# Turning K on VectorE in 32x32 blocks in a one-token decode attention layer

## The chip, the cores and the metric

The kernel runs on one NeuronCore of a Trainium2 chip. Its time is the device time of one execution in microseconds (us). A core has TensorE (PE: matmuls and, as PEld, their weight loads), VectorE (DVE), ScalarE (ACT), GpSimd (POOL) and SyncE (SP), each with its own program in order; they meet through semaphores. 16 DMA engines move data between HBM and the on-chip SBUF; matmuls write to the eight banks of PSUM.

## What is computed

Two tokens (batch B = 2) attend over a window of the last W = 2048 of 8192 cached positions, with 16 query heads on 8 key heads of width 256. The result is gated by a small two-layer network. Cut to what matters:

```python
xn = layernorm(x)                                  # x: 2 x 1 x 448, all bfloat16
q = (xn @ wq).reshape(B, 1, 16, 256)               # wq: 448 x 4096
k, v = k_cache[:, :, -2048:], v_cache[:, :, -2048:]  # 2 x 8 x 2048 x 256, two query heads each
p = softmax(q @ k.T * 256 ** -0.5)
s = (p @ v).reshape(B, 1, 4096) @ wo               # wo: 4096 x 448
g = silu(relu(xn @ w1) @ w2)                       # w1: 448 x 1792, w2: 1792 x 448
out = x + s * g
```

## The kernel before

The work is cut into four units (u = 0 to 3), each one token and four key heads. K of a unit and V of a unit are 4 MB each; a partition holds NT = 64 positions of one head with 256 values each, 32 partitions to a head. Every load is issued by SP, in this order: two rows' share of wq, K0, the rest of wq, K1, V0, w1, w2, and, as buffers come free, K2, V1, K3, V2, V3 in two parts (`load_v` with cuts at 48 and 64 of 64), then wo in the parts of `WO_PARTS` (L106, L530; 32 groups of rows in all). There are two buffers each for K and V; `load_k` (L206) waits for the last transpose of the unit two before, `load_v` (L209) for its last PV matmul (V1 for q's matmuls), since wq lies in a V buffer and wo in a K buffer.

The program is laid out by hand: each helper appends operations to the lists of the engines, and the order of the calls (L510 to the end) is the order on each engine. Semaphore waits follow from the dependencies given.

- `do_T` (L294) turns K for the score matmuls: 16 chunks a unit, each four TensorE transposes of 128x128 4-byte words (two bfloat16 each) into a PSUM bank, moved to `kt` by DVE (L309) or, for 7 of 16, ACT (L311).
- `do_S` (L313) makes the scores in bank `sbk`: 32 matmuls a unit, in groups of four that lie side by side on the array, each with the stationary `qz` (32 columns) and a moving operand of 512 columns. All heads' queries meet all rows, and what doesn't belong is masked later.
- `softmax` (L326): maximum over each row (`rm4`), a mask for other heads' columns (`far`, giving `rmm`), maximum again (`rm`), the maximum per head by a small transpose on TensorE (`mrow`, `mall`, `bias`), the shift by it with a second mask (`s_sb`, L351), exp on ACT (`e_sb`, sum in `ssum`), four transposes on TensorE, a copy to `pt`, and the reciprocal of the sum (`gs` matmul, `rs`).
- `do_PV` (L378) multiplies `pt` with V: 32 matmuls a unit, for unit u-1 put into the gaps of unit u's softmax by `gaps` (L499). `idle_work` (L481) puts filler matmuls into the gaps whose result nobody reads. `attend_scale`, `attend_turn` and `attend_spread` (L391 to L411) scale the result (`o_sb`), turn it (`at_exp`) and write it as the stationary `at_z` of the last product.
- `do_q` (L418) makes q once K0 has been turned. `do_H`, `do_hT`, `do_F` (L441 to L463) are the gating network, between units 1 and 2.
- At the end 128 matmuls of 8x112 (four for each of 32 row groups of wo) add up in `obk`, two DVE operations apply the gate and the residual, and ACT issues the store.

Matmuls are issued by one helper, so most of them have the line L281.

Of the kernel before, what the change touches and what calls it, by code (L numbers as in the profile page):

```python
# [76 lines left out]
def bass_recurrent_scan__sliding_block_cached__dense_activation_relu__decode_kernel(  # L77
# [23 lines left out]
    NCHUNK = NT // 4  # L101
# [4 lines left out]
    WO_PARTS = [8, 8, 6, 4, 4, 2]  # L106
# [5 lines left out]
    NTB = 5  # L112
    ON_ACT = (1, 3, 5, 8, 10, 12, 14)
    FAR = -1.0e30
    LOW = -30000.0

    es = contextlib.ExitStack()
    with es:
# [18 lines left out]
        own = named("own", [128, 4], F32)  # L137
        far = named("far", [128, 4], F32)
        low4 = named("low4", [128, 4], F32)
        low = named("low", [128, 512], F32)  # L140
        fold = named("fold", [128, 32], BF)
        fold16 = named("fold16", [128, NWO], BF)
        fold8 = named("fold8", [128, 8], F32)
# [9 lines left out]
        qz = named("qz", [128, 2 * NU * 64], BF)  # L153
        h_n = named("h_n", [128, FC // 4], BF)
        h_z = named("h_z", [128, 14 * GAP], BF)
# [5 lines left out]
        rm4 = named("rm4", [128, 4], F32)  # L161
        rmm = named("rmm", [128, 4], F32)
# [4 lines left out]
        s_sb = named("s_sb", [128, 512], F32)  # L167
        e_sb = named("e_sb", [128, 512], BF)
# [9 lines left out]
        kt = [named(f"kt{i}", [128, 1024], BF) for i in range(NCHUNK)]  # L178

        tb = [psum(f"tb{i}", [128, 1024], BF) for i in range(NTB)]  # L180
        sbk = psum("sbk", [128, 512], F32)
        obk = psum("obk", [128, 512], F32)
        mb16 = psum("mbk", [128, 1024], BF)
        mbk = mb16[:, :].bitcast(F32).tensor
# [48 lines left out]
        p_qz = pr.op(POOL, lambda e: e.memset(qz[:, :], 0.0), [p_one])  # L233
        p_z = [pr.op(POOL, lambda e, t=t: e.memset(t[:, :], 0.0)) for t in (h_z, at_z)][-1]

        a_z = [pr.op(ACTE, lambda e, t=t: e.memzero(t[:, :])) for t in (obk,)][-1]
# [26 lines left out]
        def fold16_op(e):  # L263
            with nc.allow_low_precision("zeros and ones"):
                return e.tensor_reduce(out=fold16[:, :], in_=view(ident, 0, [[1, NWO], [NWO, 8]]), axis=AX.X, op=ALU.add)
        v_fold16 = pr.op(DVE, fold16_op)
        v_f8 = pr.op(DVE, lambda e: e.tensor_reduce(
            out=fold8[:, :], in_=view(ident, 0, [[1, 8], [8, 16]]), axis=AX.X, op=ALU.add))
        v_own = pr.op(DVE, lambda e: e.tensor_reduce(
            out=own[:, :], in_=view(fold8, 0, [[2, 4], [1, 2]]), axis=AX.X, op=ALU.add), [v_f8])  # L270
        v_far = pr.op(DVE, lambda e: e.tensor_scalar(
            out=far[:, :], in0=own[:, :], scalar1=1.0, scalar2=-FAR, op0=ALU.subtract, op1=ALU.mult), [v_own])
        v_low4 = pr.op(DVE, lambda e: e.tensor_scalar(
            out=low4[:, :], in0=own[:, :], scalar1=1.0, scalar2=-LOW, op0=ALU.subtract, op1=ALU.mult), [v_own])
        v_low = pr.op(DVE, lambda e: e.tensor_copy(
            view(low, 0, [[4, 128], [1, 4]]), view(low4, 0, [[0, 128], [1, 4]])), [v_low4])
        v_gs = pr.op(DVE, lambda e: e.tensor_copy(
            view(gsum, 0, [[8, 16], [1, 8]]), view(fold8, 0, [[0, 16], [1, 8]])), [v_f8])
# [11 lines left out]
        st["mbk"] = v_xr  # L290

        evac, last_S = {}, {}

        def do_T(u, i):  # L294
            n_th = NCHUNK * u + i
            bank, src = tb[n_th % NTB], kbuf[u % 2]
            src_f, bank_f = src[:, :].bitcast(F32), bank[:, :].bitcast(F32)
            deps = [d_k[u], p_idf, evac.get(n_th - NTB)]
            for n in range(4):
                lo = (4 * i + n) * (DH // 2)  # L300
                o = pr.op(PE, lambda e, n=n, lo=lo: e.matmul(  # L301
                    bank_f[:, n * 128:(n + 1) * 128], lhsT=src_f[:, lo:lo + 128], rhs=ident_f[:, :],
                    start=True, stop=True, is_transpose=True), deps)
                deps = []
            st["T", u] = o
            dst = kt[i]
            deps = [o, last_S.get(n_th - NCHUNK)]
            if i not in ON_ACT:
                evac[n_th] = pr.op(DVE, lambda e: e.tensor_copy(dst[:, :], bank[:, :]), deps)  # L309
            else:  # L310
                evac[n_th] = pr.op(ACTE, lambda e: e.activation(dst[:, :], bank[:, :], ACT.Copy), deps)  # L311

        def do_S(u, g):  # L313
            deps = [st["q"]] + ([st.get(("shift", u - 1))] if g == 0 else [])
            for par in range(2):
                lo = 64 * (2 * u + par) + 24 - 8 * g
                for i in range(4):
                    o = pr.op(PE, mm(sbk[32 * i:32 * i + 32, :], qz[:, lo:lo + 32], view(kt[4 * g + i], par, [[2, 512]]),
                                     g == 0 and par == 0, g == 3 and par == 1, tile_position=(0, 32 * i)),
                              deps + [evac[NCHUNK * u + 4 * g + i]])  # L320
                    deps = []
            for i in range(4):
                last_S[NCHUNK * u + 4 * g + i] = o
            st["S", u] = o

        def softmax(u, fill=()):  # L326
            fill = list(fill)

            def meanwhile():
                if fill:  # L330
# [3 lines left out]
            v = pr.op(DVE, lambda e: e.tensor_reduce(  # L334
                out=rm4[:, :], in_=view(sbk, 0, [[1, 4], [4, 128]]), axis=AX.X, op=ALU.max), [st["S", u]])
            v = pr.op(DVE, lambda e: e.tensor_tensor(out=rmm[:, :], in0=rm4[:, :], in1=far[:, :], op=ALU.add), [v, v_far])
            v = pr.op(DVE, lambda e: e.tensor_reduce(out=rm[:, :], in_=rmm[:, :], axis=AX.X, op=ALU.max),  # L337
                      [v, st.get(("rmT", u - 1))])
# [4 lines left out]
                out=mrow[0:1, :], in_=view(mbk, 0, [[1, 8], [8, 16]], n=1), axis=AX.X, op=ALU.max, negate=True),  # L343
# [3 lines left out]
                view(mall, 0, [[8, 16], [1, 8]], n=1), view(mrow, 0, [[0, 16], [1, 8]], n=1)),  # L347
                [v, st.get(("bias", u - 1))])
            m = st["bias", u] = pr.op(PE, mm(mbk_ap(128, 1), mall[0:1, :], one_f[0:1, :], True, True), [v, p_one])
            v = st["mbk"] = pr.op(DVE, lambda e: e.tensor_copy(bias[:, :], mbk_ap(128, 1)), [m])  # L350
            v = st["shift", u] = pr.op(DVE, lambda e: e.scalar_tensor_tensor(  # L351
                out=s_sb[:, :], in0=sbk[:, :], scalar=bias[:, 0:1], in1=low[:, :], op0=ALU.add, op1=ALU.min),
                [v, v_low, st.get(("exp", u - 1))])
            meanwhile()
            a = st["exp", u] = pr.op(ACTE, lambda e: e.activation(  # L355
                e_sb[:, :], s_sb[:, :], ACT.Exp, accum_out=ssum[:, 0:1]),
                [v, st.get(("Pt", u - 1)), st.get(("gs", u - 1))])
            deps = [a, st["mbk"]]
            for j in range(4):
                o = pr.op(PE, lambda e, j=j: e.matmul(  # L360
                    mb16[:, 512 + 128 * j:640 + 128 * j], lhsT=e_sb[:, 128 * j:128 * j + 128],
                    rhs=ident[:, :], start=True, stop=True, is_transpose=True), deps)
                deps = []
            st["Pt", u] = o
            v = st["pt", u] = pr.op(DVE, lambda e: e.tensor_copy(  # L365
                view(pt[u % 2], 0, [[256, 2], [16, 16], [8, 2], [1, 8]]),
                view(mb16, 512, [[256, 2], [8, 16], [128, 2], [1, 8]])), [o, st.get(("PV", u - 2))])
            meanwhile()
            m = st["gs", u] = pr.op(PE, mm(mbk_ap(130, 1), gsum[:, :], ssum[:, 0:1], True, True), [v_gs, a, v])
            st["rs", u] = st["mbk"] = pr.op(DVE, lambda e: e.reciprocal(rs[:, u:u + 1], mbk_ap(130, 1)), [m])  # L370
            assert not fill

        obk_last = tb[3][:, :].bitcast(F32).tensor
# [4 lines left out]
        def do_PV(u, gs=range(4)):  # L378
            bank, src, p = out_bank(u), vbuf[u % 2], pt[u % 2]
            for g in gs:  # L380
                deps = [next(d for hi, d in d_v[u] if hi >= 16 * g + 16), st["pt", u], a_z if u < NU - 1 else st["tb3"], st["obk"] if u < NU - 1 else None]
                for a in range(2):
                    for i in range(4):
                        lo = (16 * g + 4 * i + 2 * a) * DH
                        o = pr.op(PE, mm(bank[32 * i:32 * i + 16, :],
                                         p[:, 256 * a + 64 * i + 16 * g:256 * a + 64 * i + 16 * g + 16], src[:, lo:lo + 2 * DH],
                                         g == 0 and a == 0, g == 3 and a == 1, tile_position=(0, 32 * i)), deps)
                        deps = []
            st["PV", u] = o
# [28 lines left out]
        def do_q():  # L418
# [10 lines left out]
            deps = [v, v_xr]  # L429
            for n in range(4):  # L430
                o = pr.op(PE, lambda e, n=n: e.matmul(
                    mb16[:, 128 * n:128 * n + 128], lhsT=view(q_n, 256 * (n // 2) + n % 2, [[2, 128]]),
                    rhs=ident[:, :], start=True, stop=True, is_transpose=True), deps)
                deps = []
            for b in range(2):
# [45 lines left out]
        def idle_work(n):  # L481
            wbk = tb[2][:, :].bitcast(F32).tensor
            deps = [st["q"], p_id]
            for _ in range(n):
                pr.op(PE, mm(view(wbk, 0, [[1, 512]]), ident[:, :], qz[:, :], True, True), deps)
                deps = []
# [106 lines left out]
```

## Time and profile before

| | us |
|---|---|
| median of 13 runs | 112.37 (112.11 to 113.86) |
| the profiled execution | 112.13 |
| its span (first to last instruction) | 110.3 |
| PE busy / PEld busy | 79.4 / 55.1 |
| DVE busy / ACT busy | 49.4 / 35.9 |

The profile is of one execution. The span is cut into 40 slices; a row has one digit for each, the busy share in tenths. A group of instructions is named by line, engine, operation and out<-in tiles; behind the bar stand its busy time, the mean duration of one in ns, and the engine's idle time just before it with what ended it. Matmuls overlap, so their durations are longer than their spacing. "The chain" follows the work that ended last back through what released each step. From the same trace come the records of when each transfer's last piece had landed, and of the TensorE clock that the throttle granted (1.0 or 0.5; mean 0.967 here).

### The profile page before, as it was taken

The numbers are of one execution on the slowest core, as the hardware profiler recorded it, in microseconds if no ns is written. First come the engines' busy times: TensorE is split into PE (matmuls) and PEld (weight loads), VectorE is DVE, ScalarE is ACT, GpSimd is POOL, SyncE is SP. The second block draws the span as 40 slices with busy tenths as digits, with TensorE's granted clock in tenths as the row PEclk, the third lists the DMA queues.
The fourth block names the chain that finished last, engine by engine and source line by source line (L and its number), as shares of the span: only waits on it lengthen the run. The fifth ranks groups of instructions, "written<-read, shape, count | busy, mean of one in ns | idle before, by whom it ended". The sixth has DMA issues, their size and how long they took to land.

```text
span 110.3 us, 1971 instructions
## 1 busy us (share of the span) xinstructions
PE 79.4 (72%) x867; PEld 55.1 (50%) x867; DVE 49.4 (45%) x114; ACT 35.9 (33%) x44; POOL 2.3 (2%) x12
## 2 busy tenths in 40 slices
PE   0010039998766999858489999857399985898991
PEld 0000039993312977323389877322397741335881
DVE  2292005485254575464400976463256655454001
ACT  4930004685002468402000858302046771200000
POOL 6200000000000000000000000000000000000000
PEclk9999999999999999999958999999859999999999
DMA  3989989998999899999999999999999999999930
GB/s 72 500 380 463 475 361 453 493 416 380 416 505 404 380 416 418 404 491 416 478 428 386 428 475 416 386 463 463 392 416 463 395 428 416 385 424 414 395 138 7
DMA packets 2908, 44.24 MB, mean 401 GB/s; under 512 B 338, under 2 KB 468, under 8 KB 1364
## 3 DMA queue, kind: packets, MB, share of 16 engines
q1 hardware_dynamic: 2864, 44.11, 94.4%
q8 instruction: 7, 0.11, 0.4%
q10 hardware_dynamic: 36, 0.01, 0.0%
q14 instruction: 1, 0.01, 0.0%
HBM read 44.11 MB, written 0.00 MB: 400 GB/s over the span
## 4 chain that ended last, share of the span: by engine, by line
PE 40%; DMA 37%; DVE 14%; SPq 3%; ACT 2%; issue 2%
DMA kbuf<-in_A_wo_dram 24%; PE tb L301 20%; DMA kbuf<-in_A_k_cache_dram 13%; PE sbk L281 6%; PE obk L281 4%; PE tb L281 4%; SPq L36 3%; DVE kt L309 2%; PE mbk L281 2%; DVE s_sb L351 2%; ACT e_sb L355 2%; DVE rm L334 2%; PE mbk L360 1%; DVE mrow L342 1%; PE mbk L339 1%
## 5 line engine op out<-in xcount | busy, mean ns | idle before, releaser
L301 PE MATMUL tb<-ident_f,kbuf 128*128 128x128 f32 x256 | 35.8, 300 | 10.6 <-DMA kbuf<-in_A_k_cache_dram 10.6
L301 PEld LDWEIGHTS tb<-ident_f,kbuf 128*128 128x128 f32 x256 | 32.0, 156 | 15.0 <-DMA kbuf<-in_A_k_cache_dram 10.7
L311 ACT ACTIVATE kt<-tb 128x1024 bf16<-128x1024 bf16 x28 | 27.4, 1023 | 26.9 <-PE tb L301 26.7
L309 DVE COPY kt<-tb 128x1024 bf16<-128x1024 bf16 x36 | 24.7, 690 | 23.3 <-PE tb L301 23.1
L281 PE MATMUL sbk<-kt,qz 128*32 128x512 bf16 x128 | 11.0, 393 | 1.6 <-DVE kt L309 1.1
L355 ACT ACTIVATE e_sb<-s_sb 128x512 bf16<-128x512 f32 x4 | 2.5, 629 | 21.4 <-DVE s_sb L351 21.4
L281 PE MATMUL obk<-vbuf,pt 128*16 128x512 bf16 x96 | 7.4, 379 | 0.0
L281 PE MATMUL obk<-kbuf,at_z 128*8 128x112 bf16 x128 | 7.0, 213 | 0.4 <-DMA kbuf<-in_A_wo_dram 0.2
L281 PEld LDWEIGHTS obk<-kbuf,at_z 128*8 128x8 bf16 x128 | 6.3, 87 | 1.0 <-DMA kbuf<-in_A_wo_dram 0.9
L281 PE MATMUL tb<-qz,ident 128*128 128x512 bf16 x20 | 6.2, 382 | 0.0
L281 PEld LDWEIGHTS sbk<-kt,qz 128*32 128x32 bf16 x128 | 2.7, 94 | 5.4 <-DVE kt L309 2.1
L281 PE MATMUL mbk<-ident,xg 2*128 2x2 bf16 x7 | 0.3, 164 | 6.6 <-DVE xg L246 6.6
L334 DVE TENSOR_REDUCE rm<-sbk 128x4 f32<-128x512 f32 x4 | 2.8, 692 | 4.3 <-PE sbk L281 4.3
L281 PE MATMUL tb<-wf,h_z 128*8 128x112 bf16 x56 | 4.3, 260 | 0.5 <-DVE h_z L460 0.5
L281 PEld LDWEIGHTS tb<-wf,h_z 128*8 128x8 bf16 x56 | 4.2, 110 | 0.5 <-issue 0.5
L365 DVE COPY pt<-mbk 128x512 bf16<-128x512 bf16 x4 | 1.7, 424 | 5.0 <-PE mbk L360 5.0
L281 PEld LDWEIGHTS mbk<-ident,xg 2*128 2x128 bf16 x7 | 0.3, 101 | 6.6 <-DVE xg L246 6.6
L474 ACT ACTIVATE ea<-tb 8x112 f32<-8x112 f32 x1 | 0.3, 253 | 9.0 <-PE tb L281 9.0
L339 PE MATMUL mbk<-ident_f,rm 128*1 128x128 f32 x4 | 1.1, 270 | 2.9 <-DVE rm L337 2.9
L351 DVE SCALAR_TENSOR_TENSOR s_sb<-sbk,bias,low 128x512 f32<-128x512 f32 x4 | 3.0, 751 | 0.1
L556 DVE TENSOR_TENSOR tmp<-obk,g_sb 8x112 f32<-8x112 f32 x1 | 0.3, 263 | 6.2 <-PE obk L281 6.2
L281 PEld LDWEIGHTS obk<-vbuf,pt 128*16 128x16 bf16 x96 | 2.1, 87 | 1.8
(77 smaller groups left out, 48.0 us busy)
## 6 DMA issues: line engine op xcount, KB each, us to landing
kbuf<-in_A_k_cache_dram SPq DMA_DIRECT2D x4, 4096.0 KB, 31.7
vbuf<-in_A_v_cache_dram SPq DMA_DIRECT2D x3, 4096.0 KB, 39.1
wf<-in_B_w_dram SPq DMA_DIRECT2D x2, 1568.0 KB, 43.8
vbuf<-in_A_v_cache_dram SPq DMA_DIRECT2D x1, 3072.0 KB, 19.3
vbuf<-in_A_wq_dram SPq DMA_DIRECT2D x1, 2560.0 KB, 19.7
kbuf<-in_A_wo_dram SPq DMA_DIRECT2D x2, 896.0 KB, 23.5
vbuf<-in_A_wq_dram SPq DMA_DIRECT2D x1, 1024.0 KB, 5.0
vbuf<-in_A_v_cache_dram SPq DMA_DIRECT2D x1, 1024.0 KB, 21.2
```

Source lines behind the costliest of these rows:

```text
L36: o = _Op(eng, lambda e: e.dma_start(dst, src), [d for d in deps if d is not None], True)
L281: return lambda e: e.matmul(out_ap, lhsT=lhsT, rhs=rhs, start=start, stop=stop, skip_group_check=True, **kw)
L301: o = pr.op(PE, lambda e, n=n, lo=lo: e.matmul(bank_f[:, n * 128:(n + 1) * 128], lhsT=src_f[:, lo:lo + 128], rhs=ident_f[:, :], start=True ...
L309: evac[n_th] = pr.op(DVE, lambda e: e.tensor_copy(dst[:, :], bank[:, :]), deps)
L311: evac[n_th] = pr.op(ACTE, lambda e: e.activation(dst[:, :], bank[:, :], ACT.Copy), deps)
L334: v = pr.op(DVE, lambda e: e.tensor_reduce(out=rm4[:, :], in_=view(sbk, 0, [[1, 4], [4, 128]]), axis=AX.X, op=ALU.max), [st["S", u]])
L339: m = st["rmT", u] = pr.op(PE, lambda e: e.matmul(mbk_ap(0, 128, 1), lhsT=rm[:, :], rhs=ident_f[:, :], start=True, stop=True, is_transpose ...
L342: v = pr.op(DVE, lambda e: e.tensor_reduce(out=mrow[0:1, :], in_=view(mbk, 0, [[1, 8], [8, 16]], n=1), axis=AX.X, op=ALU.max, negate=True) ...
L351: v = st["shift", u] = pr.op(DVE, lambda e: e.scalar_tensor_tensor(out=s_sb[:, :], in0=sbk[:, :], scalar=bias[:, 0:1], in1=low[:, :], op0= ...
L355: a = st["exp", u] = pr.op(ACTE, lambda e: e.activation(e_sb[:, :], s_sb[:, :], ACT.Exp, accum_out=ssum[:, 0:1]), [v, st.get(("Pt", u - 1) ...
L360: o = pr.op(PE, lambda e, j=j: e.matmul(mb16[:, 512 + 128 * j:640 + 128 * j], lhsT=e_sb[:, 128 * j:128 * j + 128], rhs=ident[:, :], start= ...
L365: v = st["pt", u] = pr.op(DVE, lambda e: e.tensor_copy(view(pt[u % 2], 0, [[256, 2], [16, 16], [8, 2], [1, 8]]), view(mb16, 512, [[256, 2] ...
```

## The change

K is turned by DVE instead of TensorE: four instructions a unit, each taking a quarter of the words of each position (32 of 128) for all 64 positions, and turning them in 32x32 blocks of 4-byte words, straight from `kbuf` to `kt`. A block stays in its 32 partitions, so q must stand in all four quarters: one matmul with `qrep` copies it, a DVE transpose and two products with `gmask` lay it block-diagonally into `qz` (8 columns a matmul instead of 32). The scores then hold no foreign columns, so both masks and the shift go, and exp reads PSUM with the bias. P is turned by DVE and spread over the partitions by 16 small matmuls with `spread`; a product with `hmask` writes `pt`. The gate's `h` is turned on DVE as well. q's matmuls come ahead of all else on TensorE, fillers are left out but for unit 3, and wo comes in seven parts. PSUM banks are no longer shared. Cut to its core:

```diff
-    WO_PARTS = [8, 8, 6, 4, 4, 2]
+    WO_PARTS = [9, 7, 5, 4, 3, 2, 2]
-        p_qz = pr.op(POOL, lambda e: e.memset(qz[:, :], 0.0), [p_one])
-        p_z = [... for t in (h_z, at_z)][-1]
-        a_z = [... memzero ... for t in (obk,)][-1]
+        p_z = [... for t in (mall, qrep, spread, h_z, at_z)][-1]
+        a_z = [... memzero ... for t in (obk, sbk, hbk, obk_last)][-1]
...
-            for n in range(4):
-                o = pr.op(PE, ... e.matmul(bank_f[:, n * 128:(n + 1) * 128], lhsT=src_f[:, lo:lo + 128],
-                    rhs=ident_f[:, :], start=True, stop=True, is_transpose=True), deps)
-            if i not in ON_ACT:
-                evac[n_th] = pr.op(DVE, lambda e: e.tensor_copy(dst[:, :], bank[:, :]), deps)
-            else:
-                evac[n_th] = pr.op(ACTE, lambda e: e.activation(dst[:, :], bank[:, :], ACT.Copy), deps)
+        def do_T(u, blk):
+            st["T", u] = st["kt", u, blk] = pr.op(DVE, lambda e: e.transpose(
+                view(dst, 0, [[1, 32 * NT]]), view(src, 32 * blk, [[DH // 2, NT], [1, 32]])),
+                [d_k[u], st.get(("S", u - 1, blk))])
...
+                    o = pr.op(PE, mm(sbk[32 * i:32 * i + 8, :], qz[:, lo:lo + 8],
+                                     view(kt[blk], 2 * i + par, [[64, NT], [8, 8]]),
+                                     blk == 0 and par == 0, blk == NBLK - 1 and par == 1, tile_position=(0, 32 * i)), deps)
...
             a = st["exp", u] = pr.op(ACTE, lambda e: e.activation(
-                e_sb[:, :], s_sb[:, :], ACT.Exp, accum_out=ssum[:, 0:1]),
+                e_sb, sbk[:, :], ACT.Exp, bias=bias[:, 0:1], accum_out=ssum[:, 0:1]),
-            for j in range(4):
-                o = pr.op(PE, ... e.matmul(mb16[:, 512 + 128 * j:640 + 128 * j], lhsT=e_sb[:, 128 * j:128 * j + 128], ...
+            v = st["e_t", u] = pr.op(DVE, lambda e: e.transpose(e_t, e_sb), [a, st.get(("Pt", u - 1))])
+            for x in range(4):
+                for g in range(4):
+                    lo = 128 * (4 * x + g)
+                    o = pr.op(PE, mm(view(pbk, 2 * x, [[8, 16], [1, 2]]), spread[:, lo:lo + 128],
+                                     view(et, 512 + 2 * g, [[32, 16], [1, 2]]), g == 0, g == 3), deps)
...
+            m = pr.op(PE, mm(pbk[:, :], qrep[:, :], q_n[:, :], True, True), [v, v_qr])
+            v = pr.op(DVE, lambda e: e.transpose(view(q_t, 0, [[1, 512]]), view(pbk, 0, [[64, 8], [1, 2], [2, 32]])), [m])
+            for r in range(2):
+                st["q"] = pr.op(DVE, lambda e, r=r: e.tensor_tensor(
+                    out=view(qz, r, [[64, 16], [8, 8], [2, 4]]), in0=view(q_t, 256 * r, [[1, 16], [32, 8], [0, 4]]),
+                    in1=view(gmask, 0, [[0, 16], [0, 8], [1, 4]]), op=ALU.mult), [v, v_gm])
...
+            v = pr.op(DVE, lambda e: e.transpose(h_t[:, :], view(h_n, 0, [[1, 7], [7, 32]])), [v])
...
         def scores(u):
-            for i in range(NCHUNK):
-                do_T(u, i)
-                if i >= 6 and i % 4 == 2:
-                    do_S(u, (i - 6) // 4)
+            for blk in range(NBLK):
+                do_T(u, blk)
+                if blk == 1 and u > 1:
+                    attend_turn(u - 2)
+                if blk == 2 and u > 1:
+                    attend_spread(u - 2)
+                do_S(u, blk)
...
-        softmax(0, gaps(0))
+        softmax(0)
-        softmax(1, gaps(1))
+        softmax(1, [fill(0, (0,)), fill(), fill(0, (1, 2)), fill(0, (3,))])
-        softmax(2, gaps(2))
+        softmax(2, [fill(1, (0,)), fill(), fill(1, (1, 2)), fill(1, (3,))])
-        softmax(3, gaps(3))
+        softmax(3, [fill(2, (0,)), fill(n=1), fill(2, (1, 2), 2), fill(2, (3,), 2)])
         attend_scale(2)
+        idle_work(6)
         do_PV(3, (0, 1))
```

## The prediction

> **What bounds it now.** I began with the page's slices and queue rows. In the slices each digit is the busy share of a 2.76 us slice in tenths; a queue row gives packets, MB and its packets' time as a share of 16 engines.
>
> ```profile
> DMA  3989989998999899999999999999999999999930
> q1 hardware_dynamic: 2864, 44.11, 94.4%
> q8 instruction: 7, 0.11, 0.4%
> ```
>
> The 16 DMA engines are full from the second slice to the 38th: one stream of 44.11 MB, all from SP's queue. The change moves the same bytes, so it can only win where the kernel trails the stream, and only lose where it makes the stream's consumers late. So I read the end next: the chain in order of time (start, length, what), then the timeline of the same stretch.
>
> ```profile
> 79.91 26.79 DMA kbuf<-in_A_wo_dram
> 106.70 0.04 issue
> 106.74 1.36 PE obk L281 x24
> 108.10 0.02 issue
> 108.12 0.27 DVE tmp L556
> ```
>
> ```profile
> 90.91 0.64 PE L281 MATMUL sbk<-kt,qz 128*32 128x512 bf16 x5 [0.38 <-DVE kt L309]
> ...
> 100.64 0.95 PE L281 MATMUL obk<-kbuf,at_z 128*8 128x112 bf16 x16
> ...
> 102.83 3.63 PEld L281 LDWEIGHTS obk<-kbuf,at_z 128*8 128x8 bf16 x72 [0.41 <-DMA kbuf<-in_A_wo_dram]
> ...
> 106.74 1.17 PEld L281 LDWEIGHTS obk<-kbuf,at_z 128*8 128x8 bf16 x24 [0.28 <-DMA kbuf<-in_A_wo_dram]
> ```
>
> The reader should see two things. The end follows the weights wo, but 24 matmuls (six of 32 row groups) still run after 106.7. And TensorE was hardly idle before that: 0.41 and 0.28 us of waiting. The trace's landing records say why. K of units 0 to 3 landed at 15.42, 32.51, 59.40, 78.91; wq at 21.52; the two parts of the last V at 95.93 and 98.42; the six parts of wo at 100.60, 102.79, 104.46, 105.58, 106.70, 107.26. The matmuls start 49 ns apart, four to a row group: 0.20 us a group against some 0.27 us of stream. TensorE would idle if it were not for its late start at 100.64.
>
> Last the costliest groups, for durations:
>
> ```profile
> L301 PE MATMUL tb<-ident_f,kbuf 128*128 128x128 f32 x256 | 35.8, 300 | 10.6 <-DMA kbuf<-in_A_k_cache_dram 10.6
> ...
> L311 ACT ACTIVATE kt<-tb 128x1024 bf16<-128x1024 bf16 x28 | 27.4, 1023 | 26.9 <-PE tb L301 26.7
> L309 DVE COPY kt<-tb 128x1024 bf16<-128x1024 bf16 x36 | 24.7, 690 | 23.3 <-PE tb L301 23.1
> ...
> L334 DVE TENSOR_REDUCE rm<-sbk 128x4 f32<-128x512 f32 x4 | 2.8, 692 | 4.3 <-PE sbk L281 4.3
> ```
>
> **K turned on DVE.** 256 TensorE transposes and 64 evacuations leave; 16 DVE transposes of 2048 words come. No row shows one. Near rows: the reduce above takes 692 ns for 512 words; DVE products of 28 and 128 words take 180 and 286 ns, a slope of 1.06 ns a word; the fp32 copies of 128 and 512 words (220, 426 ns) give 0.54. Bounds: 0.54 x 2048 + 150 ns = 1.25 us, and 4.5 us if a word took two passes. [...] I take 2.2 us each in a row: 16 x 2.2 = 35 us. DVE goes from 49 to about 62 us of 110: not full, but in order, so transposes and softmax of one unit now add up instead of overlapping.
>
> **TensorE's clock.** The trace's clock record has 0.5 for 3.41 us from 55.4 and from 79.3, each after a 3.4 us stretch in which PE was 0.56 and 0.41 busy; stretches of 0.60 and more kept full clock. The matmuls of the gate (tb<-wf,h_z) started 93 ns apart at half, 49 at full. Without the transposes PE has about 1 us of score matmuls per 2.2 us of DVE, so I count half clock while K is turned, full in the second half of each softmax.
>
> **Scores.** 128 matmuls stay, eight per block, four side by side: a group of four started every 238 ns before; at half clock 0.43. They read kt at every 16th byte (before every fourth). [...] Row: the weights tb<-ident,h_n were read every 14 bytes and groups of four loads of 32 columns came every 53 ns, no slower than any load. By the row nothing is lost; [...]. I take the row [...].
>
> **Softmax.** Gone: rmm, the second rm, the shift (0.16 + 0.16 + 0.75, gaps 0.1) = 1.2 us and e_sb's four transposes (0.4). Added: a DVE transpose of 512 elements (nearest: the reduce, 0.7), 16 small matmuls (four 128-column transposes started 55 ns apart, so 0.9 + 0.2; half clock 2.0), pt as a product with fp32 from PSUM (0.7 for 0.42). Net +0.5 at full clock, to +1.4. From the scores' end to rs it was 5.4 us; now 6.0 to 6.9.
>
> **The order of DVE, from landing to landing.** T0 15.46 + 8.8 = 24.3. q: seven groups at half clock from 21.52, 24.9; q_n 0.7, one matmul 0.4, transpose 0.7, two products 1.4: 28.1 (qz was ready at 28.7). Scores 3.6: 31.7; softmax 6.5: 38.2. K1 has waited since 32.5. T1 8.8: 47.0; last block 1.1; softmax 6.2: 54.3; o_sb 0.7; H beside it 0.9; h_n, h_t, h_z 1.0 (28 matmuls for one transpose, even); gate matmuls 2.9 at full clock; its tail 1.7 as before: 61.0. K2 landed at 59.4. T2 8.8 + 0.5 for at_exp and at_z: 70.3; 1.1; softmax 6.2; o_sb 0.7: 78.3. K3 lands at 78.91: **0.6 us to spare**. T3 9.3: 88.2; last block 1.1: 89.3 (was 91.55). pt 5.05 + 0.5 and 0.4 for a half-clock part: 95.2 (was 96.63). PE then has eight PV matmuls, two fillers, gs (1.3) and six fillers (1.3): 97.1 to begin the last PV, which began at 97.00; 2.4 + 1.2 us as before: 100.7. A gain of 1.4 us in the softmax is spent on fillers, which cost nothing while V's second part (98.42) and wo are late anyway.
>
> **wo in seven parts.** Fitting the six landing steps gives 0.27 us a group + 0.02 a part. Nine groups land at 100.88, the last at 107.28. TensorE starts at 100.9, has 31 groups' work of 6.3 us and a 0.2 us interlude until then, so it catches up; after 107.28 only the last two groups' eight matmuls remain: 0.04 + 7 x 0.049 + 0.21 = 107.88, against 108.08. **Gain 0.20 us.**
>
> **At nothing.** SP: K2 needs T0 (24.3), V1 q's matmuls (24.9), K3 T1 (47), V2 the first PV (54), V3 the second (77.5); each stands before its predecessor has landed (V2 at 88.62, 11 us cover for V3); wo's seventh issue is 0.43 us beside that. Were the cover gone, the stream would stop. POOL's three memsets (spread 2.1 us by qz's 0.52 for a quarter) and the two DVE copies are done near 9 us, ACT's three memzeros put xr back by 1.7 us: all before 15.4, when nothing but wq is awaited. Less evacuation on ACT frees nothing: it was off the path.
>
> **Sum.** Profiled execution 112.13 (span 110.3 and 1.8 around it) - 0.20 = 111.93. The median is 0.24 above that execution; where runs scatter because TensorE trails in the last stretch, this ends, so I keep a third of it: **112.0 us**. What a measurement of this kernel can tell from no change is about 0.3%, 0.34 us; this forecast lies at that edge.
>
> **Rivals.**
> - *The DVE queue is late for K3* (slower, 0.30). All 16 transposes and four softmaxes are in one line with 0.6 us to spare. If the gate's 56 matmuls run at half clock, 56 x 0.044 = 2.5 us come ahead of T2; T3 begins 1.9 late, the wo matmuls at 102.6, with 6.7 us of work of their own: 109.3 or, with fillers at half clock too, 110. That is 113.4 to 114.2; I say 113.9. It decides from 0.7 us of lateness, or 0.05 us per transpose. For it: PE was 0.56 busy in the stretch before the gate even with the old work. Against: scores, PV, spread and H now fall close together there.
> - [...]
> - *A word takes two passes*, so the turn isn't cheaper (0.03): 16 x 2.2 more, all but the first few serial: about 145.
> - *The stream itself ends earlier* (faster, 0.10). The seven 16 KB instruction fetches (q8) each held one DMA engine for about 1.05 us, and the first, at 30.4, fell on the engine that was last already: its lag on the next grew from 0.21 to 1.28 us. There are 613 matmuls for 867, so some five fetches; if the first hits another engine, landings come up to 0.2 earlier: 111.7.
> - The likeliest case has 0.52 and its own range is 111.7 to 112.3.
>
> **Chances.** Faster: 0.31 of the likeliest case and 0.09 of the stream's. Same: 0.19 and 0.01 of these, 0.06 of the late queue. The rest is slower. The range goes down to the earlier stream and up past the late queue, leaving out the two dear rivals and a few in a hundred at each end: 111.6 to 114.9.
>
> **What would show it.** kt<-kbuf at 2.2 us each and T3 within 0.1 us of K3's landing; pt of unit 3 near 95; eight matmuls, not 24, after the last landing near 107.3. Wrong if T3 starts late, if wo's matmuls start after 101.2, or if the granted clock is 0.5 in the gate or after 99.

## The result, and the profile after

The changed kernel took **117.46 us** in the median (11 runs, 113.72 to 117.90) against 112.43 before (48 runs). Its executions fall into two groups, five at 113.7 to 114.6 and six at 117.5 to 117.9; the ratio on record, 1.0149 (95% interval 1.0114 to 1.0185), compares the first group alone with the quicker executions of before. The profiled execution is of that group: 114.54 us, span 112.6. The forecast was 112.0, with a range from 111.6 to 114.9: a small gain was expected, and a loss came.

The stream first: slices, and the queues' rows, of the changed kernel.

```profile
DMA  3989989989989989998998998999999998999500
```

```profile
q1 hardware_dynamic: 3008, 44.11, 92.6%
q8 instruction: 5, 0.08, 0.3%
```

It is about as full as before, and its last part lands at 107.47 by the landing records (107.26 before). So 0.2 of the 2.4 us by which the profiled executions differ can lie in the stream; the rest lies behind it. The chain of the page now runs through TensorE and DVE, where wo's transfer had stood with 24%:

```profile
PE 40%; DVE 34%; DMA 17%; ACT 3%; issue 2%; SPq 1%
DVE kt L292 20%; DMA vbuf<-in_A_wq_dram 17%; PE sbk L274 15%; PE obk L274 10%; PE mbk L274 3%; ACT et L331 3%; PE pbk L274 3%; PE fbk L274 3%; DVE et L334 3%; DVE rm L315 2%; PE obk_last L274 2%; PE wbk L274 2%; PE hbk L274 1%; DVE o_sb L368 1%; DVE qz L408 1%
```

The groups show where it came from: the scores and the transposes after, and the scores before.

```profile
L274 PE MATMUL sbk<-kt,qz 128*8 128x512 bf16 x128 | 31.1, 1071 | 14.2 <-DVE kt L292 12.0
L292 DVE STREAM_TRANSPOSE kt<-kbuf 128x2048 f32<-128x2048 f32 x16 | 35.9, 2283 | 4.9 <-DMA kbuf<-in_A_k_cache_dram 4.9
```

```profile
L281 PE MATMUL sbk<-kt,qz 128*32 128x512 bf16 x128 | 11.0, 393 | 1.6 <-DVE kt L309 1.1
```

The transposes are as forecast. The scores are not: the same 128 matmuls had 11.0 us of busy time before (393 ns each); now they have 31.1 and 1071. The timeline of unit 0 shows their beat in the weight loads: one group of four every 0.90 us.

```profile
28.01 7.37 PE L274 MATMUL sbk<-kt,qz 128*8 128x512 bf16 x32 [2.18 <-DVE qz L408]
28.89 0.12 PEld L274 LDWEIGHTS sbk<-kt,qz 128*8 128x8 bf16 x4 [0.78 <-issue]
29.79 0.12 PEld L274 LDWEIGHTS sbk<-kt,qz 128*8 128x8 bf16 x4 [0.78 <-issue]
30.69 0.12 PEld L274 LDWEIGHTS sbk<-kt,qz 128*8 128x8 bf16 x4 [0.78 <-issue]
31.59 0.12 PEld L274 LDWEIGHTS sbk<-kt,qz 128*8 128x8 bf16 x4 [0.78 <-issue]
32.49 0.12 PEld L274 LDWEIGHTS sbk<-kt,qz 128*8 128x8 bf16 x4 [0.78 <-issue]
```

The clock record has half clock from 27.8 to 31.2 and full clock from there to 38.0. The beat is 0.90 in both, so the array's clock doesn't set it. The timeline of unit 3 and the last product shows what it leads to at the other end:

```profile
82.02 4.50 DVE L292 STREAM_TRANSPOSE kt<-kbuf 128x2048 f32<-128x2048 f32 x2
...
91.42 2.01 PE L274 MATMUL sbk<-kt,qz 128*8 128x512 bf16 x8 [0.31 <-DVE kt L292]
...
103.73 0.95 PE L274 MATMUL obk<-kbuf,at_z 128*8 128x112 bf16 x16
...
104.72 5.67 PE L274 MATMUL obk<-kbuf,at_z 128*8 128x112 bf16 x112
```

K3 landed at 79.05, but DVE came to it (T3, the transposes of unit 3) at 82.02. TensorE began the last product at 103.73 (100.64 before), and its 112 matmuls no longer wait for wo at all: their own pace, to 110.4, sets the end.

### The profile page after: what moved, and what is told of

It reads as the page before. It is cut to its first block, busy times and chain, and to the rows that moved or that the text cites. A ratio compares the mean times of both kernels' runs of the same rounds, so it can differ in the third digit from the quotient of the medians.

```text
span 112.6 us, 1423 instructions
## 1 busy us (share of the span) xinstructions
PE 65.0 (58%) x621; PEld 22.8 (20%) x621; DVE 61.3 (54%) x86; ACT 9.7 (9%) x18; POOL 3.8 (3%) x14
## 4 chain that ended last, share of the span: by engine, by line
PE 40%; DVE 34%; DMA 17%; ACT 3%; issue 2%; SPq 1%
DVE kt L292 20%; DMA vbuf<-in_A_wq_dram 17%; PE sbk L274 15%; PE obk L274 10%; PE mbk L274 3%; ACT et L331 3%; PE pbk L274 3%; PE fbk L274 3%; DVE et L334 3%; DVE rm L315 2%; PE obk_last L274 2%; PE wbk L274 2%; PE hbk L274 1%; DVE o_sb L368 1%; DVE qz L408 1%
## 5 line engine op out<-in xcount | busy, mean ns | idle before, releaser
L274 PE MATMUL sbk<-kt,qz 128*8 128x512 bf16 x128 | 31.1, 1071 | 14.2 <-DVE kt L292 12.0
L292 DVE STREAM_TRANSPOSE kt<-kbuf 128x2048 f32<-128x2048 f32 x16 | 35.9, 2283 | 4.9 <-DMA kbuf<-in_A_k_cache_dram 4.9
L274 PE MATMUL obk<-vbuf,xr 128*4 128x512 bf16 x28 | 3.0, 611 | 13.2 <-DMA vbuf<-in_A_wq_dram 13.2
L315 DVE TENSOR_REDUCE rm<-sbk 128x1 f32<-128x512 f32 x4 | 2.8, 692 | 13.8 <-PE sbk L274 13.8
L331 ACT ACTIVATE et<-sbk,bias 128x512 bf16<-128x512 f32 x4 | 2.8, 688 | 76.3 <-DVE bias L328 76.3
L334 DVE STREAM_TRANSPOSE et<-et 128x512 bf16<-128x512 bf16 x4 | 2.8, 712 | 3.4 <-ACT et L331 3.4
L343 DVE TENSOR_TENSOR pt<-pbk,hmask 128x512 bf16<-128x512 f32 x4 | 2.8, 692 | 3.0 <-PE pbk L274 3.0
L274 PE MATMUL fbk<-wf,h_z 128*8 128x112 bf16 x56 | 2.9, 213 | 1.4 <-DVE h_z L423 1.4
L274 PE MATMUL wbk<-q_n,ident 128*128 128x512 bf16 x13 | 3.6, 381 | 0.0
L274 PEld LDWEIGHTS fbk<-wf,h_z 128*8 128x8 bf16 x56 | 2.8, 87 | 1.8 <-issue 1.8
```

Source lines behind the costliest of these rows:

```text
L274: return lambda e: e.matmul(out_ap, lhsT=lhsT, rhs=rhs, start=start, stop=stop, skip_group_check=True, **kw)
L292: st["T", u] = st["kt", u, blk] = pr.op(DVE, lambda e: e.transpose(view(dst, 0, [[1, 32 * NT]]), view(src, 32 * blk, [[DH // 2, NT], [1, 3 ...
L315: v = pr.op(DVE, lambda e: e.tensor_reduce(out=rm[:, :], in_=sbk[:, :], axis=AX.X, op=ALU.max), [st["S", u, NBLK - 1], st.get(("rmT", u - ...
L331: a = st["exp", u] = pr.op(ACTE, lambda e: e.activation(e_sb, sbk[:, :], ACT.Exp, bias=bias[:, 0:1], accum_out=ssum[:, 0:1]), [v, st.get(( ...
L334: v = st["e_t", u] = pr.op(DVE, lambda e: e.transpose(e_t, e_sb), [a, st.get(("Pt", u - 1))])
L343: v = st["pt", u] = pr.op(DVE, lambda e: e.tensor_tensor(out=view(pt[u % 2], 0, [[8, NT], [2, 4], [1, 2]]), in0=view(pbk, 0, [[2, NT], [0, ...
```

## The experiments

Theory 1: the step of 16 bytes between the elements of the scores' moving operand costs, at any clock. Theory 2: the DVE queue and the half clock make K late, the step is the smaller part.

**Neighbouring words.** Each group of four takes eight words in a row instead of every fourth, and the spread of P takes the same order.

```diff
-    view(kt[blk], 2 * i + par, [[64, NT], [8, 8]])
+    view(kt[blk], 16 * i + par, [[64, NT], [2, 8]])
-    view(spread, 0, [[512, 4], [160, 4], [4, 8], [1, 4]])
+    view(spread, 0, [[512, 4], [160, 4], [1, 8], [8, 4]])
```

> The changed kernel, but each group of score matmuls takes eight neighbouring words (a step of 4 bytes) instead of every fourth (16 bytes), and the spread's pattern follows. Theory 1 (the step of the moving operand costs: a group of four takes 0.90 us at either clock): groups go back to 0.24 us at full and 0.43 at half clock, the 32 of unit 0 from 7.4 to 2 to 3.6 us, T3 starts within 0.7 us of K3's landing at 79, and the time is 111.7 to 112.6. Theory 2 (the DVE queue and the half clock make K3 late, the step is the smaller part): the groups may be quicker, but T3 starts at 80.5 or later and the time stays over 113.

112.29 us (22 runs, 112.12 to 112.72), ratio 0.9973 (0.9951 to 0.9994). The timeline of unit 0's scores:

```profile
28.19 3.59 PE L274 MATMUL sbk<-kt,qz 128*8 128x512 bf16 x32 [2.18 <-DVE qz L408]
```

The 7.37 us became 3.59, T3 began at 79.73 with K3 landed at 79.12, and the loss was gone. This holds although that execution had half clock from 63.5 to 94.3 and its gate, at half clock but for its end, took 4.79 us:

```profile
56.13 4.79 PE L274 MATMUL fbk<-wf,h_z 128*8 128x112 bf16 x56 [1.40 <-DVE h_z L423]
...
79.73 4.49 DVE L292 STREAM_TRANSPOSE kt<-kbuf 128x2048 f32<-128x2048 f32 x2
```

So Theory 1 holds as to the cause.

**A step of 8 bytes**, for the size of it. The spread keeps its old order, so P's weights meet the wrong positions and only the time is read:

```diff
+    view(kt[blk], 32 * (i // 2) + 2 * (i % 2) + par, [[64, NT], [4, 8]])
```

> The changed kernel with a step of 8 bytes in the scores' moving operand; the spread is left as it was, so the weights meet the wrong positions and only the time is read. Theory 1: the cost grows with the step, so a group lies between 0.24 and 0.90 us, near 0.45 [...]. Theory 2: no difference from a step of 4 bytes, 0.43 at half clock.

One execution, 112.20 us.

```profile
28.07 3.95 PE L274 MATMUL sbk<-kt,qz 128*8 128x512 bf16 x32 [2.18 <-DVE qz L408]
```

That is 0.47 a group: about half of 16 bytes' 0.90, and a little over the 0.43 of a group with 4 bytes at half clock. Half clock from 28.2 to 31.6 and full clock behind it made no difference.

**The operand's step by itself**, in a tail of matmuls behind the last product whose results nobody reads.

```diff
+        for tiles in (4, 1):
+            for step in (1, 2, 4, 8, 16, 32):
+                idle_work(4)
+                ... 16 x mm(pbk[p0:p0 + 8, :], qz[:, 0:8], view(vbuf[1], 2 * i, [[step, 512]]), ...)
```

> The changed kernel with a tail added whose results nobody reads: after the last product, 16 matmuls each for steps of 2, 4, 8, 16, 32 and 64 bytes in the moving operand of 512 columns, first four side by side on the array, then all on one quarter, four fillers ahead of each. Theory 1: side by side, a group of four takes 0.22 to 0.24 us at 2 and 4 bytes and about 0.9 at 16, and not much more at 32 and 64, [...]; on one quarter a matmul takes 0.22 us up to 16 bytes if it is the four streams together that are too much, and more if one stream alone is. Theory 2: all steps take 0.22 to 0.24 a group at full clock.

The timeline of that tail (199.41 us in all), first four side by side at 2, 4, 8 and 16 bytes, then on one quarter at 2, 4, 8 and 16; the fillers between are left out:

```profile
110.42 1.04 PE L274 MATMUL pbk<-vbuf,qz 128*8 128x512 bf16 x16
...
112.36 1.09 PE L274 MATMUL pbk<-vbuf,qz 128*8 128x512 bf16 x16
...
114.35 1.98 PE L274 MATMUL pbk<-vbuf,qz 128*8 128x512 bf16 x16
...
117.23 3.77 PE L274 MATMUL pbk<-vbuf,qz 128*8 128x512 bf16 x16
...
131.25 3.62 PE L274 MATMUL pbk<-vbuf,qz 128*8 128x512 bf16 x16
...
135.77 3.79 PE L274 MATMUL pbk<-vbuf,qz 128*8 128x512 bf16 x16
...
140.46 7.39 PE L274 MATMUL pbk<-vbuf,qz 128*8 128x512 bf16 x16
...
148.75 14.56 PE L274 MATMUL pbk<-vbuf,qz 128*8 128x512 bf16 x16
```

Sixteen matmuls are four groups side by side, but sixteen in a row on one quarter. The medians from start to start, in us:

| step, bytes | 2 | 4 | 8 | 16 | 32 | 64 |
|---|---|---|---|---|---|---|
| a group of four, side by side | 0.216 | 0.226 | 0.45 | 0.90 | 0.92 | 0.86 |
| one matmul on one quarter | 0.215 | 0.226 | 0.45 | 0.90 | 0.92 | 0.86 |

One stream alone pays as much as four, so it isn't their number. The clock halved at 152.9, among the sixteen of 16 bytes on one quarter, and they kept 0.90. The cost doubles from 4 to 8 and to 16 bytes and then stops growing. 0.90 us over 512 elements is 1.76 ns each; 8 bytes give 0.88 and 4 bytes 0.44. All three are 1.76 ns for each 16 bytes of address touched. At full clock two elements in 16 bytes (a step of 8) still took twice the time of four (0.45 us for 0.226), and four (a step of 4) cost 5% over eight (0.226 for 0.216). Three were not run.

**Fillers** in the softmaxes of units 0 to 2, as before had them:

```diff
-        softmax(0)
+        softmax(0, [fill(n=2), fill(n=1), fill(n=5), fill(n=1)])
...
-        softmax(1, [fill(0, (0,)), fill(), fill(0, (1, 2)), fill(0, (3,))])
+        softmax(1, [fill(0, (0,)), fill(n=1), fill(0, (1, 2), 2), fill(0, (3,))])
...
-        softmax(2, [fill(1, (0,)), fill(), fill(1, (1, 2)), fill(1, (3,))])
+        softmax(2, [fill(1, (0,)), fill(n=1), fill(1, (1, 2), 2), fill(1, (3,))])
```

> The changed kernel with the fillers that the kernel before had in the softmaxes of units 0 to 2 (9, 3 and 3). Theory 1: score groups stay at 0.90 us, since that is not the clock's doing; the quicker executions stay at 113.6 to 114.6, and only those of 117.5 get rarer. Theory 2: with the clock held, the gate, the spread and the scores are all quicker and the time is 112.6 or less.

113.46 us (14 runs, 113.12 to 113.82), ratio 1.0072 (1.0048 to 1.0096). The score matmuls kept their length (1077 ns median duration), T3 began at 81.06, and no execution came near 117.5. The mean granted clock lay at 0.893 to 0.939, for 0.823 to 0.924 without the fillers. So the step makes about 1 us that fillers don't remove, and with the step left in place half clock makes the rest.

**The gate's clock alone**, the step left at 16 bytes:

```diff
         do_H()
+        idle_work(6)
         do_F()
```

> The changed kernel, step of 16 bytes and all, with six fillers between the two matmul steps of the gate, where TensorE waits for DVE for 1.2 us. If the executions of 117.5 are those in which the gate's 56 matmuls find half clock (93 ns apart for 49: 2.5 us, and the spread and H beside them), they vanish and all lie at 113.6 to 114.8. If the half clock of another stage makes them (scores' last block, spread, the end), they stay at about half of all.

113.80 us (10 runs, 113.44 to 114.25), ratio 1.0100 (1.0072 to 1.0127). Six fillers, in a gap of 1.4 us in which TensorE waited for DVE, took away the group of 117.5.

**The changed kernel once more**, unedited, for a profile of an execution of that group.

> The changed kernel once more, unedited, for a profile of an execution near 117.5 us (about half of them). If that is the gate at half clock, its 56 matmuls start 93 ns apart from some 60 us on and T2 and T3 begin about 3 us later than in the profile of 114.5 (64.6 and 82.0). If another stage is at half clock, the gate takes 2.9 us as there and the 3 us appear elsewhere.

> The changed kernel unedited, as in look_a: a second chance for an execution near 117.5 us, with the same expectations of the gate and of T2 and T3.

They took 113.55 and 115.80 us. The second shows the mechanism part-way; the timeline of its gate:

```profile
60.09 4.24 PE L274 MATMUL fbk<-wf,h_z 128*8 128x112 bf16 x56 [1.41 <-DVE h_z L423]
...
65.96 2.29 DVE L292 STREAM_TRANSPOSE kt<-kbuf 128x2048 f32<-128x2048 f32 x1
```

The gate took 4.24 us for 2.91, since the clock came back only at 62.9; T2 began 1.35 later than in the profile of 114.54 us, T3 1.3 later, and the time was 1.26 longer. An execution of 117.5 itself left no profile, so its full 3 us are not itemised. Their mean granted clocks (0.823 and 0.838, against 0.848 at 114.54) say only that they had more time at half clock, by estimate 3 to 7 us (2 x (1 - clock) x span), not where. A gate wholly at half clock would be 56 x 0.044 = 2.5 us longer, an estimate from before's 93 and 49 ns between its matmuls at half and full clock; that it is the gate fits this profile and the fillers' effect, but is not shown.

**Seven parts of wo on the kernel before**, nothing else:

```diff
-    WO_PARTS = [8, 8, 6, 4, 4, 2]
+    WO_PARTS = [9, 7, 5, 4, 3, 2, 2]
```

> The kernel before with wo in the seven parts of the change and nothing else: the one term that was to bring the gain. Forecast's term: eight matmuls instead of 24 after the last landing, 0.1 to 0.3 us less. Rival: in the kernel before TensorE is as late as the stream (it starts the last product at 100.64 and waits 0.28 us in all of its last 5 us), so smaller parts find it behind anyway, and a first part of nine lands 0.27 us later: no change within 0.2 us.

112.13 us (22 runs), ratio 0.9961 (0.9935 to 0.9987), against a median of 112.44 before: a gain of 0.3 us where 0.2 was forecast, and it needs none of the rest of the change. Its end in the trace:

```profile
107.47 0.39 PEld L281 LDWEIGHTS obk<-kbuf,at_z 128*8 128x8 bf16 x8 [0.16 <-DMA kbuf<-in_A_wo_dram]
```

Eight matmuls are left after the last landing, as forecast. But that landing came at 107.43 (107.26 before), so the product of this execution ended only 0.05 us earlier; where the rest of the medians' 0.3 lies, no profile shows.

**What can be had.** Neighbouring words with the fillers; the same without them but with wo's last part halved (`[9, 7, 5, 4, 3, 2, 1, 1]`, `idle_work(2)` for `idle_work(6)`); all of these together; and the kernel before with the eight parts.

> e1_words with the fillers of e3_fillers. If what is left of the loss is the clock (score groups 0.43 at half clock, T3 at 79.7 where K3 lands at 79.1), T3 begins at K3's landing and the time is 111.9 to 112.2, all executions within 0.3. If the end now hangs on the stream alone (last landing 107.5 and eight matmuls behind it), it stays at 112.2 to 112.4.

> e1_words with wo's last part of two row groups cut into one and one, and two fillers instead of six ahead of the last PV matmuls. If the end hangs on the last landing and what follows it, four matmuls remain instead of eight: 0.2 us less than e1_words, near 112.1. If TensorE is behind by then, or an eighth part lands as much later, no change; with fewer fillers half clock may also reach the last product, which would make it 0.5 us or more slower.

> What the runs so far point to, in one kernel: neighbouring words, fillers in all units, eight parts of wo, two fillers ahead of the last PV. If the parts' gain adds to that of the fillers, 112.0 and no execution over 112.5; if the end hangs on the stream alone, the same 112.1 as e6 and e8.

> The kernel before with wo in eight parts, K still turned on TensorE: if turning K on DVE is worth nothing once its step is mended, this is as quick as e8 and e9, 112.0 to 112.1; if it is worth something, it stays at 112.2 or above.

| | median us | ratio to before (95%) |
|---|---|---|
| words + fillers (21 runs at 111.97 to 112.43, one at 246.24, unexplained) | 112.15 | 0.9965 (0.9946 to 0.9984) |
| words + eight parts | 112.11 | 0.9953 (0.9932 to 0.9974) |
| words + fillers + eight parts | 112.08 | 0.9972 (0.9964 to 0.9981) |
| before + eight parts | 112.00 | 0.9983 (0.9947 to 1.0019) |

With words and fillers T3 starts at 79.07, when K3 lands, and the time is 0.14 us less than with words alone: the end hangs on the stream. Side by side, the two edits tell what half clock costs:

| | without the fillers | with them |
|---|---|---|
| step of 16 bytes | 113.7 to 114.6, or 117.5 to 117.9 | 113.46 |
| neighbouring words (4 bytes) | 112.29 | 112.15 |

Half clock cost microseconds only where the step had used up the slack (4.0 us between the medians of 117.46 and 113.46, 0.14 with neighbouring words). With all edits together the profiled gate took 4.53 us, mostly at half clock, and the time was still 112.03.

The mended kernels beat both kernels, but turning K on DVE earns nothing that these runs can tell: the intervals overlap, and before with new parts is as quick. They scatter less, for a reason that wasn't tested: all of these together ran within 111.98 to 112.13, while before with eight parts had four of 14 executions near 113.6.

## Why the prediction was wrong

The step that failed is **Scores**, which put the wider step of the moving operand at nothing: "By the row nothing is lost", "I take the row". In its place the runs showed 0.90 us a group at either clock, for the 0.24 or 0.43 that it counted: 7.4 us instead of 3.6 for unit 0's scores, and 2.0 instead of 1.1 for the last block of each later unit. That used up the 0.6 us to spare before K3. With neighbouring words the loss was gone, half clock or not, so this step carried the rest. Three faults lie in it:

- The row was of weight loads every 14 bytes, not of a moving operand. It doesn't even exclude the same price for weights: 32 columns 14 bytes apart touch some 28 pieces of 16 bytes, by estimate 49 ns at the tail's 1.76, and the row's groups came every 53 ns.
- The row of the same kind, the scores themselves at 4 bytes, was misread. Only unit 0's first two groups start 238 ns apart; the next six came after 224 to 227 ns each, which is the tail's 0.226 at 4 bytes, where PV's contiguous operand had 216. So the read already cost a little at 4 bytes, and four times that step was put at nothing.
- A price for the wider step got a chance of 0.05 when the chain had 0.6 us to spare. The prediction had no row to read it from; the author's estimate was a group at most doubled, by the 0.43 us counted for it at half clock. It was nearly right: 8 x 0.43 = 3.4 us for unit 0 and 0.9 for each last block, where 3.8 and 0.9 came. That its total, about 117, meets the median of 117.46 is luck: the softmaxes came out about 1 us shorter than counted, so the step with some half clock in unit 1 made 114.5, and more half clock made the other 3.

Along the forecast's own line, forecast and measured starts:

| | forecast | after | difference, and its source |
|---|---|---|---|
| T0 done | 24.3 | 24.3 | |
| qz ready | 28.1 | 28.0 | |
| unit 0's scores | 3.6 long | 7.4 | +3.8, the step |
| softmax of unit 0 | 6.5 long | 5.1 | -1.4: above all spread 0.66 for 1.1 (2.0 at half clock), and gs ran beside pt |
| T1 | 38.2 | 40.5 | +2.3 |
| last block, units 1 to 3 | 1.1 each | 2.0 | +0.9 each |
| T2 | 61.0 | 64.6 | +3.6: the block, and PV and H of unit 1 at half clock (H 1.47 us, 0.84 with the fillers) |
| T3 | 78.95 | 82.0 | +3.1: the block, less a shorter softmax and the 0.65 to spare |
| last product | 100.9 | 103.7 | +2.8 |
| its end | 107.88 | 110.4 | +2.5 |

- **K turned on DVE** was right: 8.9 us for four in a row, 2.2 each, as its slope of 1.06 ns a word gives (1.06 x 2048 = 2.17 us, an estimate). DVE's busy time is 61.3 us (forecast 62).
- **The DVE queue is late** named the place and the price: with no slack left, lateness passes through almost whole (T3 3.1 us late, the last product's end 2.5). But its 113.9 counted the gate at half clock, and in the profile of 114.54 the gate ran at full clock (2.9 us); the lateness there is for the most part the step's, 111.93 + 2.5 = 114.4. Half clock's some 3 us come on top in the executions of 117.5. If they lie in the gate, as it seems, counting its matmuls at full clock as the likeliest case was the second error, in 6 of 11 executions.
- **wo in seven parts**: a gain of 0.20 forecast, 0.3 measured alone by the medians. Its sum has slips: the last landing was forecast at 107.28 and came at 107.43, and 31 groups of 6.3 us from 100.9 would end after it; it is 30 groups and 5.9, and in the run TensorE did wait 0.16 us for the last part. In the changed kernel the gain is lost, since TensorE is behind and its 112 matmuls run without a wait.
- **The stream ends earlier** did not come: there were five instruction fetches for seven, but the last landing was 0.2 later.
- Fillers ahead of the last PV were priced at nothing "while V's second part and wo are late anyway". In the profile after, V was there at 98.58 and six fillers kept PV until 100.26: that cover was gone. By estimate that is some 1.3 of the 2.5 us at the end; no run took them out with the step left at 16 bytes.

## What to carry to other kernels

Before a layout is turned into a matmul's moving operand, count how many elements of it lie in 16 bytes: from a step of 4 to 16 bytes the read took 1.76 ns for each 16 bytes it touched here, and changing which positions share a group mended it for no cost. Where a change puts stages that used to overlap into one in-order queue, add up the queue from landing to landing and price each doubtful step against the slack left, not against the whole. And test the small part of a change alone: here the split of the last load was all of the gain that the runs can tell.

## What the hardware showed that was not expected

- Moving operands: 0.226 us for 512 bfloat16 at a step of 4 bytes, 0.45 at 8, 0.90 at 16, hardly more or less at 32 and 64 (0.92, 0.86); the same for one stream as for four side by side, and the same at half and full clock from 16 bytes on. At half clock a step of 8 bytes cost little: 0.47 a group in unit 0's scores (0.45 in the tail, at full clock), for 0.43 at 4 bytes.
- A DVE transpose of 2048 4-byte words took 2.20 us from start to start, one word per 1.07 ns. Four bytes cost no more than two: 512 words took 0.72 us, 512 bfloat16 0.71.
- Sixteen matmuls of 128x32 with new 128-column weights each took 0.66 us together, in units at half and at full clock.
